# Summing one batch's fp32 log gates with fp32 matmuls, and reading the upper halves of the others as a strided view

## The chip, the cores and the metric

The kernel runs on one core of a Trainium2 chip. The metric is the device time of one execution in microseconds (us), lower is better. A time is a median over the executions named with it. "PE" is the TensorE matmul unit and "PEld" its weight loads, "DVE" is VectorE, "ACT" is ScalarE, "POOL" is GpSimd. A chunk is 128 time steps; a batch has 6 of them.

## The reference

Inputs are q, k, v and f_logit of shape 4 x 8 x 768 x 48 (batch, heads, time, head dimension), and four weight matrices. A gated linear attention is followed by an MLP mixer:

```python
f = 1.0 / (1.0 + np.exp(-f_logit))
state = np.zeros((B, H, D, D))
for t in range(S):
    state = f[:, :, t, :, None] * state + np.einsum('bhd,bhe->bhde', k[:, :, t], v[:, :, t])
    y[:, :, t] = np.einsum('bhd,bhde->bhe', q[:, :, t], state)
x = y.transpose(0, 2, 1, 3).reshape(4, 768, 384)

h = np.maximum(x.transpose(0, 2, 1) @ w_tok1, 0.0) @ w_tok2      # token mixing, 768 -> 256 -> 768
u = x + h.transpose(0, 2, 1)
h2 = np.maximum(u @ w_ch1, 0.0) @ w_ch2                          # channel mixing, 384 -> 1536 -> 384
return u + h2
```

## The kernel before

The attention is done in chunks. With L = -log f, each chunk needs the prefix sums of L over its 128 steps (one matmul with an upper triangular matrix of ones) and, for every head dimension, the total over the chunk (a matmul with a column of ones). Both are sums of fp32 numbers, and PE takes longer for them in fp32. So the kernel splits L into a bf16 high half and a bf16 rest and sums the two into the same fp32 PSUM tile.

The gates of one group of chunks: one Exp, one Ln rounded to bf16, the same Ln again in fp32, and a subtraction on POOL or DVE, whichever the planner finds free.

```python
def gates(b, c0, c1, key):
    ...                                          # cut: views fb (fp32), hi and lo (bf16)
    a = add({"ACT": cost}, lambda e: nc.scalar.activation(fb, fb, AF.Exp, bias=0.0, scale=-1.0), ...)
    h = add({"ACT": cost}, lambda e: nc.scalar.activation(hi, fb, AF.Ln, bias=1.0, scale=1.0), ...)
    g = add({"ACT": cost}, lambda e: nc.scalar.activation(fb, fb, AF.Ln, bias=1.0, scale=1.0), key, [h])
    o = add({"POOL": 0.85 * n, "DVE": 0.4 * n + 0.08},
            lambda e: on(e).tensor_tensor(lo, fb, hi, ALU.subtract), key, [g, h])
```

The sums of one chunk. In the totals, the tile of L is the *stationary* operand (`lhsT`), and is loaded as weights (L280 below: a load of 128 x 128 before each matmul), for one column of output:

```python
def cumsum(e):
    ...                                          # cut: a PSUM bank; Sv are its first 384 columns
    nc.tensor.matmul(Sv, lhsT=tri_bf, rhs=Lhi[i][:, c, :, 0:D], start=True, stop=False)
    nc.tensor.matmul(Sv, lhsT=tri_bf, rhs=Llo[i][:, c, :, 0:D], start=False, stop=True)
    if c < NCH - 1:
        bh, bl = blk(Lhi[i][:, c]), blk(Llo[i][:, c])
        for hp in range(HP):                     # 4 pairs of heads
            o = pS[:, DM + hp:DM + hp + 1]
            nc.tensor.matmul(o, lhsT=bh[:, hp, :], rhs=ones_bf, start=True, stop=False)
            nc.tensor.matmul(o, lhsT=bl[:, hp, :], rhs=ones_bf, start=False, stop=True)
```

From these sums come decays exp(-S) and exp(S) for q and k, then transposes of both on PE, scores, a mask, the state update, and the readout (`py`) of y. The mixer follows: token mixing (`x_bf`, `h1T`), the tiles of u, their transposes (`uT`), and the two long channel matmuls (`pm<-uT` and `pm<-w_ch,zT`).

Nothing is issued in the order of the program text. Each operation is added to a plan with a guessed cost per engine, and `Plan.order()` simulates the engines greedily and fixes every engine's order before the kernel runs. That an engine waits in its order can be seen at POOL, which stood idle for 8.10 us before one subtraction, with loads behind it (below).

## Time and profile before

| | before |
|---|---|
| time, median of 4 runs (beside the changed kernel) | 193.61 us (193.45 to 193.84) |
| span of the profiled run | 192.0 us |
| PE busy | 170.5 us, 89% |
| DVE busy, ACT busy | 129.5 and 129.4 us, 67% each |
| readout of batch 0 ends | 31.8 us |
| first matmul from `uT` (channel mixing of batch 0) | 42.6 us |

The page of the profiled run, cut to the lines used here. The first is each engine's busy time. The rows show the busy share in 40 slices of 4.8 us, in tenths, and PEclk the granted PE clock, in tenths of full speed.

```profile
span 192.0 us, 4351 instructions
...
PE 170.5 (89%) x1668; PEld 105.4 (55%) x1668; DVE 129.5 (67%) x286; ACT 129.4 (67%) x292; POOL 81.0 (42%) x92
...
PE   0787896679999999999999899999998999999992
...
PEclk9999999957999999999999999999999999999999
```

PE is nearly full after slice 8, so whatever delays its long matmuls shows in the end time, and PE has holes only before. The clock row reads half only in slice 8.

The chain of waits, cut to pieces (start, length, what):

```profile
14.08 0.55 DVE Llo_80 L261
...
15.88 0.46 PE py L371 x7
...
21.14 0.46 PE py L371 x7
...
31.23 0.35 PE py L371 x7
...
101.08 6.33 DMA kT_92<-kh_88
```

The clock records in the packed trace begin at 24.8 us, and the row prints time without a record as 9. Where a time is from "the clock records", these are meant.

Two lines of the timeline (start, length, engine, line, what; in brackets the wait before and what ended it), a copy on DVE during POOL's two subtractions:

```profile
38.00 1.74 DVE L190 CAST u_bf<-u_nat_109 128x384 bf16<-128x384 f32 x1
...
37.89 3.34 POOL L261 TENSOR_TENSOR Llo_81<-f_sb_77,Lhi_79 128x768 bf16<-128x768 f32 x2 [8.10 <-ACT f_sb_77 L259]
```

The same copy, undisturbed, takes 0.35 us at 36.22 us. POOL had waited 8.10 us for ACT's Ln, with loads queued behind it in its order.

The groups of the sums (line, engine, operation, operands, shapes, count, then busy us and mean ns of one):

```profile
L461 PE MATMUL pm<-uT,w_ch_68 128*128 128x384 bf16 x288 | 54.5, 330 | 1.1 <-ACT zT L194 0.8 <-DVE zT L196 0.2
...
L274 PE MATMUL pS<-Lhi_79,tri_bf 128*128 128x384 bf16 x12 | 4.3, 358 | 0.0
...
L280 PEld LDWEIGHTS <-Lhi_78 128*128 128x128 bf16 x40 | 3.2, 103 | 2.8 <-issue 2.4
```

A weight load of a bf16 tile takes about 0.10 us. In steady flow it hides behind the matmuls: the second channel matmuls (L480) have 288 loads of 98 ns, 27.3 us in all, and PE is idle for 0.0 us before them.

### The profile page before, as it was taken

The page shows a single profiled execution, that of the slowest core. Times are in us where ns is not written, and L with a number is a line of the kernel's source. Part 1 is how long each engine was busy: PE and PEld are TensorE (multiplying, and loading weights), DVE is VectorE, ACT ScalarE, POOL GpSimd, SP SyncE. Part 2 cuts the span into 40 slices and gives each one's busy share as a digit, 9 for nine tenths or more (in the row PEclk, how much of TensorE's full clock was granted, in tenths as well). Part 3 has the DMA queues.
Part 4 walks back from the last instruction along what each step waited for, and adds up shares of the span by engine and source line. Part 5 has one row for each costly group of instructions (what it writes and reads, how often), then busy time and mean ns, then how long its engine had stood idle before and what let it go on. Part 6 is the DMA issues. An engine that isn't in the chain of part 4 may idle for free.

```text
span 192.0 us, 4351 instructions
## 1 busy us (share of the span) xinstructions
PE 170.5 (89%) x1668; PEld 105.4 (55%) x1668; DVE 129.5 (67%) x286; ACT 129.4 (67%) x292; POOL 81.0 (42%) x92
## 2 busy tenths in 40 slices
PE   0787896679999999999999899999998999999992
PEld 0455553346666666656555566565665654656560
DVE  4578888988899757988998973898673637200222
ACT  4999793987989959774899953257996122598000
POOL 7999992199992449993990300000000000000000
PEclk9999999957999999999999999999999999999999
DMA  8999999999999999999999343344532124310222
GB/s 105 162 149 143 141 216 194 196 101 107 112 192 195 167 122 171 180 199 155 180 144 115 58 82 113 103 85 130 84 64 48 41 85 100 78 70 2 81 86 82
DMA packets 102213, 23.23 MB, mean 121 GB/s; under 512 B 95312, under 2 KB 100992, under 8 KB 102192
## 3 DMA queue, kind: packets, MB, share of 16 engines
q0 software_dynamic: 78800, 13.77, 99.6%
q1 hardware_dynamic: 23392, 9.18, 21.1%
q8 instruction: 13, 0.21, 0.5%
q14 instruction: 8, 0.07, 0.1%
HBM read 25.17 MB, written 4.72 MB: 156 GB/s over the span
## 4 chain that ended last, share of the span: by engine, by line
PE 53%; DVE 18%; ACT 15%; DMA 6%; issue 4%; POOL 2%; DVEq 0%; POOLq 0%; ACTq 0%
PE pm L480 24%; PE pm L461 14%; DMA kT_92<-kh_88 3%; PE pm L407 3%; DMA k_sb_72<-in_k_dram 3%; PE pm L426 2%; ACT zT L194 2%; DVE u_bf L190 2%; PE py L371 1%; ACT state_bd_103 L188 1%; DVE Am_96 L337 1%; DVE Am_95 L337 1%; DVE u_nat_109 L430 1%; ACT u_bf L188 1%; ACT state_bd_102 L188 1%
## 5 line engine op out<-in xcount | busy, mean ns | idle before, releaser
L461 PE MATMUL pm<-uT,w_ch_68 128*128 128x384 bf16 x288 | 54.5, 330 | 1.1 <-ACT zT L194 0.8
L480 PE MATMUL pm<-w_ch_69,zT 128*128 128x384 bf16 x288 | 50.5, 326 | 0.0
L194 ACT ACTIVATE zT<-pm 128x384 bf16<-128x384 f32 x73 | 34.7, 500 | 6.2 <-PE pm L461 5.8
L480 PEld LDWEIGHTS <-zT 128*128 128x128 bf16 x288 | 27.3, 98 | 17.7 <-issue 0.4
L461 PEld LDWEIGHTS <-w_ch_68 128*128 128x128 bf16 x288 | 26.3, 98 | 17.2 <-issue 2.6
L237 POOL DMA_DIRECT2D k_sb_72<-in_k_dram x12 | 11.0, 920 | 4.9 <-DMA f_sb_76<-in_f_logit_dram 4.9
L237 POOL DMA_DIRECT2D q_sb_70<-in_q_dram x12 | 11.2, 932 | 4.4 <-DMA w_ch_69<-in_moe_w_ch_dram 3.6
L196 DVE TENSOR_SCALAR zT<-pm 128x384 bf16<-128x384 f32 x23 | 12.2, 551 | 1.2 <-PE pm L461 1.2
L237 POOL DMA_DIRECT2D k_sb_73<-in_k_dram x12 | 11.2, 932 | 3.7 <-DVE zT L196 3.7
L426 PE MATMUL pm<-h1T,w_tok_67 128*128 128x384 bf16 x48 | 10.9, 332 | 0.8 <-ACT h1T L194 0.4
L237 POOL DMA_DIRECT2D v_sb_75<-in_v_dram x12 | 11.3, 941 | 0.0
L237 POOL DMA_DIRECT2D v_sb_74<-in_v_dram x12 | 11.1, 926 | 0.4 <-issue 0.4
L237 POOL DMA_DIRECT2D q_sb_71<-in_q_dram x12 | 11.2, 936 | 0.0
L261 POOL TENSOR_TENSOR Llo_81<-f_sb_77,Lhi_79 128x768 bf16<-128x768 f32 x3 | 5.0, 1669 | 14.7 <-ACT f_sb_77 L259 14.7
L489 DVE TENSOR_TENSOR out_sb_114<-u_nat_110,pm 128x384 f32<-128x384 f32 x2 | 1.1, 550 | 14.1 <-PE pm L480 14.1
L274 PE MATMUL pS<-Lhi_78,tri_bf 128*128 128x384 bf16 x12 | 4.9, 409 | 4.8 <-POOL ident masks.py:197 4.8
L188 ACT CAST x_bf_106<-py 128x384 bf16<-128x384 f32 x10 | 4.8, 482 | 6.4 <-PE py L376 6.4
L190 DVE COPY x_nat_105<-py 128x384 f32<-128x384 f32 x8 | 4.5, 558 | 6.5 <-ACT x_bf_107 L188 6.4
L188 ACT CAST x_bf_107<-py 128x384 bf16<-128x384 f32 x8 | 3.9, 488 | 7.3 <-PE py L376 7.2
L190 DVE COPY x_nat_104<-py 128x384 f32<-128x384 f32 x9 | 5.0, 558 | 5.4 <-ACT x_bf_106 L188 5.4
L287 ACT ACTIVATE G_82<-pS 128x384 bf16<-128x384 f32 x12 | 5.9, 488 | 4.2 <-PE pS L281 4.1
L430 DVE TENSOR_TENSOR u_nat_109<-x_nat_104,pm 128x384 f32<-128x384 f32 x12 | 6.2, 550 | 3.6 <-PE pm L426 3.5
(237 smaller groups left out, 394.8 us busy)
## 6 DMA issues: line engine op xcount, KB each, us to landing
f_sb_77<-in_f_logit_dram POOLq DMA_DIRECT2D x2, 1152.0 KB, 12.1
f_sb_76<-in_f_logit_dram SPq DMA_DIRECT2D x6, 192.0 KB, 4.5
q_sb_70<-in_q_dram POOLq DMA_DIRECT2D x12, 96.0 KB, 5.7
k_sb_72<-in_k_dram POOLq DMA_DIRECT2D x12, 96.0 KB, 5.2
v_sb_74<-in_v_dram POOLq DMA_DIRECT2D x12, 96.0 KB, 5.2
w_ch_68<-in_moe_w_ch_dram POOLq DMA_DIRECT2D x1, 1152.0 KB, 15.5
q_sb_71<-in_q_dram POOLq DMA_DIRECT2D x12, 96.0 KB, 7.9
k_sb_73<-in_k_dram POOLq DMA_DIRECT2D x12, 96.0 KB, 6.1
```

What stands on the lines that cost most here:

```text
L188: nc.scalar.copy(dst, src)
L190: on(e).tensor_copy(dst, src)
L194: nc.scalar.activation(dst, src, AF.Relu, bias=0.0, scale=1.0)
L196: nc.vector.tensor_scalar(dst, src, 0.0, None, ALU.max)
L237: lambda e, dst=dst, src=src: nc.gpsimd.dma_start(out=dst[i][:, c], in_=chunk_of(src, b, c)),
L261: lambda e: on(e).tensor_tensor(lo, fb, hi, ALU.subtract), key, [g, h])
L287: return lambda e: nc.scalar.activation(dst.rearrange("t h d -> t (h d)"), t["pS"][:, 0:DM], AF.Exp, bias=0.0, scale=scale)
L407: nc.tensor.matmul(t["p"][:, 0:DM], lhsT=w_tok1[:, kt, rt * 128:(rt + 1) * 128], rhs=x_bf[i][:, kt, :], start=(kt == 0), stop=(kt == NCH - 1))
L426: nc.tensor.matmul(t["p"][:, 0:DM], lhsT=w_tok2[:, kt, tt * 128:(tt + 1) * 128], rhs=h1T[:, kt, :], start=(kt == 0), stop=(kt == 1))
L430: u = made["u", b, tt] = add({"DVE": 0.47}, lambda e, tt=tt, t=t: nc.vector.tensor_tensor(u_nat[i][:, tt, :], x_nat[i][:, tt, :], t["p"][: ...
L461: nc.tensor.matmul(t["p"][:, 0:384], lhsT=w_ch1[:, kt, cc * 128:(cc + 1) * 128], rhs=uT[:, kt, th * 384:(th + 1) * 384], start=(kt == 0), ...
L480: nc.tensor.matmul(t["p"][:, 0:DM], lhsT=zT[:, kt, tt * 128:(tt + 1) * 128], rhs=w_ch2[:, kt, :], start=(kt == 0), stop=(kt == NCC - 1))
```

## The change

The intent: drop the second Ln and, in batch 0, the subtraction too.

- One Ln writes L in fp32. The bf16 high half is not computed but *read*: a bf16 view of the fp32 tile with stride 2 picks the upper 16 bits. In batches 1 to 3 the rest is still computed and summed.
- In batch 0, where PE has holes, L is summed in fp32, without a split.
- The planner's costs are retuned, so the order of everything changes. It also puts filler matmuls (`warm`, whose result nobody reads) into gaps that it foresees on PE before 46 us, meant to keep the clock up. Two more chunks have q and k transposed by PE rather than by DMA, and `x_bf` is copied from `x_nat` in SBUF.

```diff
+    L = two([128, NCH, H, 64], FP32, "L")
+    Lhi = [tl.bitcast(BF16).rearrange("t c h (d two) -> t c h d two", two=2)[:, :, :, :, 1] for tl in L]
...
-        h = add({"ACT": cost}, lambda e: nc.scalar.activation(hi, fb, AF.Ln, bias=1.0, scale=1.0), ...)
-        g = add({"ACT": cost}, lambda e: nc.scalar.activation(fb, fb, AF.Ln, bias=1.0, scale=1.0), key, [h])
-        o = add({"POOL": 0.85 * n, "DVE": 0.4 * n + 0.08},
-                lambda e: on(e).tensor_tensor(lo, fb, hi, ALU.subtract), key, [g, h])
+        g = add({"ACT": cost}, lambda e: nc.scalar.activation(full, fb, AF.Ln, bias=1.0, scale=1.0), ...)
+        o = g if b == 0 else add({"POOL": 0.85 * n} if b == 3 else {"DVE": 0.4 * n + 0.08},
+                lambda e: on(e).tensor_tensor(lo, full, hi, ALU.subtract), key, [g])
...
+            if b == 0:
+                nc.tensor.matmul(Sv, lhsT=tri_f, rhs=L[i][:, c, :, 0:D], start=True, stop=True)
+                if c < NCH - 1:
+                    bl = blk(L[i][:, c])
+                    for hp in range(HP):
+                        nc.tensor.matmul(pS[:, DM + hp:DM + hp + 1], lhsT=bl[:, hp, :], rhs=ones_f,
+                                         start=True, stop=True)
+                return
...
-        s = made["S", b, c] = add({"PE": 0.56}, cumsum, key - 0.02,
+        s = made["S", b, c] = add({"PE": 0.56 if b else 1.1}, cumsum, key - 0.02,
...
-        made["xb", b, c] = add(either, lambda e: copy(e, x_bf[i][:, c, :], t["py"][:, 0:DM]), ...)
+        made["xb", b, c] = add({"DVE": 0.28, "ACT": 0.38}, lambda e: copy(e, x_bf[i][:, c, :], x_nat[i][:, c, :]), ...)
...
-    XBAR_QK = 16
+    XBAR_QK = 18
...
+    def warm(reps):
+        def fn(e):
+            p = bank("mix", "warm")
+            for _ in range(reps):
+                nc.tensor.matmul(p[:, 0:DM], lhsT=idle[:, 0:128], rhs=idle, start=True, stop=True)
```

Cut: the planner's code that sizes the fillers, a separate planner queue for DMA transposes, the clearing of the new tiles, smaller cost constants, and batch 1's gates, which are computed one chunk at a time instead of two and planned a little later.

More of the change, by code (lines that the diff above doesn't have):

```diff
@@ L15 @@
 class Plan:
-    LATE = {"PE": 0.32, "ACT": 0.24, "DVE": 0.24, "POOL": 0.3, "SP": 0.1, "Q": 2.0}
+    LATE = {"PE": 0.32, "ACT": 0.24, "DVE": 0.24, "POOL": 0.3, "SP": 0.1, "Q": 2.0, "X": 1.3}
     BANKS = {"att": 5, "mix": 3}
     WINDOW = 150
+    WARM = None
+    WARM_UNTIL = 46.0
     def __init__(self):
@@ L36, in order @@
         queues = {e: sorted((o for o in self.ops if e in o["eng"]), key=lambda o: o["key"])
-                  for e in ("PE", "ACT", "DVE", "POOL", "SP", "Q")}
+                  for e in ("PE", "ACT", "DVE", "POOL", "SP", "Q", "X")}
         free = dict.fromkeys(queues, 0.0)
@@ L80, in order @@
             t, o, e = best
+            if e == "PE" and self.WARM and free["PE"] < self.WARM_UNTIL and t - free["PE"] > 0.45:
+                t_, last = max(free["PE"], 1.3), taken["mix"][-self.BANKS["mix"]:]
+                held = self.ops[last[0]]["readers"] if len(last) == self.BANKS["mix"] else []
+                if all(r in ends for r in held):
+                    t_ = max([t_] + [visible[r] for r in held])
+                    one = 0.165 if t_ > 4.0 else 0.34
+                    reps = int((t - t_ - 0.1) * 0.8 / one)
+                    if reps > 0:
+                        w = self.add({"PE": one * reps}, self.WARM(reps), 0.0, bank="mix")
+                        taken["mix"].append(w)
+                        ends[w] = free["PE"] = t_ + one * reps
+                        visible[w], on[w] = ends[w], "PE"
+                        out.append((t_, "PE", self.ops[w]))
             n = o["n"]
@@ L83, in order @@
             visible[n] = ends[n] + self.LATE[e]
+            if e == "X" and free["Q"] > t:
+                visible[n] += 3.5
             on[n] = e
@@ L132 @@
     ones_bf = st([128, 1], BF16, "ones_bf")
+    idle = st([128, DM], BF16, "idle")
+    nc.vector.memset(idle, 0.0)
     nc.vector.memset(ones_bf, 1.0)
+    tri_f = st([128, 128], FP32, "tri_f")
+    ones_f = st([128, 1], FP32, "ones_f")
+    nc.vector.memset(ones_f, 1.0)
     tri4 = tri_bf.unsqueeze(1).broadcast_to((128, 4, 128))
@@ L145 @@
     f_sb = two([128, H, NCH, D], FP32, "f_sb")
-    Lhi = two([128, NCH, H, 64], BF16, "Lhi")
+    L = two([128, NCH, H, 64], FP32, "L")
     Llo = two([128, NCH, H, 64], BF16, "Llo")
@@ L165 @@
     out_sb = [st([128, DM], FP32, f"out_sb{n}") for n in range(NCH)]
-    for tl in (*Lhi, *Llo):
+    Lhi = [tl.bitcast(BF16).rearrange("t c h (d two) -> t c h d two", two=2)[:, :, :, :, 1] for tl in L]
+    for tl in (*L, *Llo):
         nc.vector.memset(tl[:, :, :, D:64], 0.0)
@@ L227, in load_f @@
         else:
-            m = swdge(lambda e: nc.gpsimd.dma_start(out=f_sb[i], in_=src), key, 2.28, 5.9, 0.3,
-                      [made.get(("lo", b - 2, c)) for c in range(NCH)], at)
+            m = swdge(lambda e: nc.gpsimd.dma_start(out=f_sb[i], in_=src), key, 2.28, 6.3, 0.3,
+                      [made.get(("ln", b - 2, c)) for c in range(NCH)], at)
             for c in range(NCH):
@@ L237, in load_qkv @@
                 lambda e, dst=dst, src=src: nc.gpsimd.dma_start(out=dst[i][:, c], in_=chunk_of(src, b, c)),
-                key, 0.89, 0.71, 1.0, [made.get((u, b - 2, c)) for u in users], at)
+                key, 0.89, 0.78, 1.0, [made.get((u, b - 2, c)) for u in users], at)
     def load_w(name, dst, src, key, us, units):
@@ L246, in crossbar @@
         n = add({"SP": 1.2}, lambda e: nc.sync.dma_start_transpose(out=dst, in_=src), key, deps)
-        return add({"Q": 0.7}, None, key, [n])
+        return add({"X": 0.1}, None, key, [n])
     def gates(b, c0, c1, key):
@@ L252, in gates @@
         fb = f_sb[i].rearrange("t h c d -> t c h d")[:, c0:c1]
+        full = L[i][:, c0:c1, :, 0:D]
         hi, lo = Lhi[i][:, c0:c1, :, 0:D], Llo[i][:, c0:c1, :, 0:D]
@@ L256, in gates @@
                 key, [made["f", b, c] for c in cs])
-        h = add({"ACT": cost}, lambda e: nc.scalar.activation(hi, fb, AF.Ln, bias=1.0, scale=1.0),
+        g = add({"ACT": cost}, lambda e: nc.scalar.activation(full, fb, AF.Ln, bias=1.0, scale=1.0),
                 key, [a] + [made.get(("S", b - 2, c)) for c in cs])
-        g = add({"ACT": cost}, lambda e: nc.scalar.activation(fb, fb, AF.Ln, bias=1.0, scale=1.0), key, [h])
-        o = add({"POOL": 0.85 * n, "DVE": 0.4 * n + 0.08},
-                lambda e: on(e).tensor_tensor(lo, fb, hi, ALU.subtract), key, [g, h])
+        o = g if b == 0 else add({"POOL": 0.85 * n} if b == 3 else {"DVE": 0.4 * n + 0.08},
+                lambda e: on(e).tensor_tensor(lo, full, hi, ALU.subtract), key, [g])
         for c in cs:
+            made["ln", b, c] = g
             made["lo", b, c] = o
@@ L276, in cumsum @@
             if c < NCH - 1:
-                bh, bl = blk(Lhi[i][:, c]), blk(Llo[i][:, c])
+                bh = Lhi[i][:, c].rearrange("t (hp par) dd -> t hp (par dd)", par=2)
+                bl = blk(Llo[i][:, c])
                 for hp in range(HP):
@@ L381, in attention @@
         either = {"ACT": 0.38, "DVE": 0.47}
-        made["xb", b, c] = add(either, lambda e: copy(e, x_bf[i][:, c, :], t["py"][:, 0:DM]),
-                               key + 0.03, [made.get(("t1", b - 2))], frees=y)
-        made["xn", b, c] = add(either, lambda e: copy(e, x_nat[i][:, c, :], t["py"][:, 0:DM]),
-                               key + 0.03, [made.get(("u", b - 2, c))], frees=y)
+        xn = made["xn", b, c] = add(either, lambda e: copy(e, x_nat[i][:, c, :], t["py"][:, 0:DM]),
+                                    key + 0.03, [made.get(("u", b - 2, c))], frees=y)
+        made["xb", b, c] = add({"DVE": 0.28, "ACT": 0.38}, lambda e: copy(e, x_bf[i][:, c, :], x_nat[i][:, c, :]),
+                               key + 0.03, [xn, made.get(("t1", b - 2))])
     def mixing(b, key0, span):
@@ L491, in mixing @@
                 kk, [half, made.get(("out", tt))], frees=first)
-            s = add({"SP": 0.1}, lambda e, tt=tt, o=o: nc.sync.dma_start(out=out_b[tt], in_=o), kk, [n])
+            s = add({"SP": 0.45}, lambda e, tt=tt, o=o: nc.sync.dma_start(out=out_b[tt], in_=o), kk, [n])
             made["out", tt] = add({"Q": 0.7}, None, kk, [s])
@@ L506, in masks @@
         make_upper_triangular(nc, tri_bf, val=1.0, diag=True)
+        make_upper_triangular(nc, tri_f, val=1.0, diag=True)
         make_identity(nc, ident)
@@ L510 @@
         load_qkv(0, c, 0.1 * c)
-    load_w("w_tok1", w_tok1, moe_w_tok1, 0.60, 3.0, 0.75)
+    load_w("w_tok1", w_tok1, moe_w_tok1, 0.60, 3.3, 0.75)
     load_w("w_tok2", w_tok2, moe_w_tok2, 0.61, 2.2, 0.25)
@@ L528 @@
                     load_qkv(b + 1, c, b + 0.05 + 0.1 * c)
-            n = 2
+            n = 2 if b else 1
             for c in range(0, NCH, n):
-                gates(b + 1, c, c + n, b + 0.85 + LEAD[0] + LEAD[1] * c)
+                gates(b + 1, c, c + n, b + (0.85 if b else 0.95) + LEAD[0] + LEAD[1] * c)
                 for a in range(c, c + n):
@@ L534 @@
         mixing(b, b + 1.0, 1.0)
+    def warm(reps):
[3 more added lines that the diff above has]
+                nc.tensor.matmul(p[:, 0:DM], lhsT=idle[:, 0:128], rhs=idle, start=True, stop=True)
+        return fn
+    plan.WARM = warm
     order = plan.order()
```

## The prediction

> **What bounds it now.** Three stretches, read from engine activity by window and the timeline.
> (1) 0 to 31.5 us, batch 0's attention: ACT and DVE share the load, 75 to 97% and 81 to 85% busy from 10 to 30 us. POOL issues 18 q/k/v loads at 0.93 us each; DMA is full too.
> (2) 31.5 to 46 us: PE runs out of work (57% busy from 30 to 40 us), waiting on DVE for tiles of u and on DMA: batch 1's f_logit lands at 34.0 us, w_ch1 at 39.3 us. One u_bf copy takes 1.74 us on DVE under two POOL subtractions (3.34 us in sum; alone it takes 0.35). The granted clock is 0.50 from 38.3 to 45.6 us. [...]
> (3) From 46 us PE is 97% busy, but not all is work: the 288 matmuls from uT occupy 189 ns each, against 162 where nothing holds them (72 in 11.70 us, chain of waits at 165 us). PSUM evictions by the crowded ACT and DVE hold them.
>
> **What changes.**
> - One Ln per gate group goes: 6 of 0.52 us in batch 0, 0.83 us per two chunks after. ACT loses about 11 us, 3.1 of it in stretch 1.
> - Batch 0 loses its subtractions (4 DVE of 0.56, 2 POOL of 0.98 us). Batch 1's move to DVE (6 of 0.56), so no POOL work blocks the loads from 37.9 to 41.2 us or slows the copies.
> - Batch 0's sums become fp32: estimate 0.6 to 1.0 us per chunk against 0.55, on an idle PE.
> - x_bf is copied from SBUF (about 0.35 against 0.48 to 0.56 us), after x_nat.
> - The diff also carries filler matmuls in PE gaps foreseen before 46 us, and two more chunks transposed by PE instead of DMA: about +1 us of PE, but the 6.3 us DMA piece of the chain ending at 107 us goes.
> - Strided high halves: I expect no cost in matmul or weight load.
>
> **On the path.** Stretch 1: 6.4 us less on two engines, so it should end near 29 us. This doesn't pass through whole, because w_ch1 still lands at 38.5 to 39.3 us. But the two late tok2 pairs and first sums (1.8 us at full clock) get done before, and the long matmuls start 3 us sooner. A warm clock saves 2.7 us more (5.4 us at half rate); the order shows only one filler between u and the batch-1 sums, so I count half. Sum about 4.5 us. Later: ACT relief returns perhaps 1.5 us of the held matmuls (7.7 us held in all), less 1 us for transposes.
>
> Predicted 188.3 us, 80% range 184.5 to 191.5. Faster by over 2%: 0.74; within 2%: 0.23; slower: 0.03.
>
> **What would show it.** Readout of batch 0 ending near 29 us; first matmul from uT near 39 us (now 42.6); a clock of 1.00, or a dip under 4 us, between 36 and 46 us; POOL issuing loads from 34 us without a hole; ACT busy near 118 us (129.4), DVE level; matmuls from uT below 189 ns; strided sums at 160 to 165 ns.
>
> **What would make it wrong.** Fillers or fp32 sums delaying PE's real work in stretch 1; ACT, in order, blocked on batch 1's f_logit ahead of u copies; the clock falling anyway; strided reads slowing 18 sums by 160 ns each (+3 us); a new order leaving PE holes after 46 us.

The sum: about 4.5 us (3 us, and half of 2.7 us for the clock), then 1.5 us more and 1 us less, 5 us in all. The 2.7 us are worked out from the trace (5.4 us of PE work at a granted clock of 0.50); that fillers keep the clock up was assumed. The 0.6 to 1.0 us for fp32 sums is an estimate of mine that names no trace; the trace after has 1.5 to 3.14 us per chunk.

## The result, and the profile after

| | before | after |
|---|---|---|
| time, median of 4 runs | 193.61 us | 199.55 us (199.18 to 202.96; the last slow) |
| span of the profiled run | 192.0 us | 197.4 us |
| PE busy, PE idle | 170.5, 21.5 us | 181.5, 15.9 us |
| readout of batch 0 ends | 31.8 us | 37.4 us (predicted 29) |
| first matmul from `uT` | 42.6 us | 46.8 us (predicted 39) |

The change makes the kernel slower: 1.030 times the time before, 95% interval 1.028 to 1.032. A ratio here and below is the mean time of one kernel's fast runs over the mean of the fast runs of the kernel before in the same rounds, so it is not quite the ratio of the medians. The kernel before is run again in every batch of experiments, and its median there was between 193.7 and 194.2 us.

The page after:

```profile
span 197.4 us, 4449 instructions
...
PE 181.5 (92%) x1732; PEld 114.2 (58%) x1732; DVE 127.2 (64%) x287; ACT 124.9 (63%) x287; POOL 79.2 (40%) x92
...
PE   4999999678999999989998599999779999999992
...
PEclk9999999999999999999999999999999999999999
```

DVE and ACT got their relief, and PE has 5.6 us less idle time (21.5 - 15.9). But it has 11.0 us more busy time, so the span grew by 5.4 (the fillers are 12.1 us of the busy time, so this sum alone does not name a cause). The clock row shows no dip any more, and the clock records have full rate from 17.3 us on. PE has holes near 35 to 49 us (slices 7 to 9), near 110 us (slice 22) and from 138 to 148 us (slices 28 and 29); before, slices 9 and 28 and 29 were full.

The chain of waits after, cut:

```profile
5.21 1.65 PE pS L301 x2
6.86 1.50 PE pS L305 x8
8.35 0.98 PE warm L576 x3
...
18.38 0.84 PE pS L301 x2
19.22 0.79 PE pS L305 x8
...
27.06 1.73 PE warm L576 x10
...
33.02 0.35 PE py L406 x7
...
105.58 1.34 DVE state_105 L393
...
107.31 1.46 DVE state_bd_107 L215
...
142.85 3.95 DMA qT_96<-qh_92
```

The sums of batch 0 are now *in* the chain. L301 is the fp32 prefix sum, which the trace shows as two instructions. L305 is the totals: four matmuls, eight instructions, 1.50 us for four numbers per partition. One chunk's sums take 3.14 us (5.21 to 8.35), later 1.63 (0.84 + 0.79). The fillers are in the chain as well.

The groups of the sums after:

```profile
L496 PE MATMUL pm<-uT,w_ch_73 128*128 128x384 bf16 x288 | 53.1, 326 | 2.5 <-DVE zT L221 2.5
...
L576 PE MATMUL warm<-idle 128*128 128x384 bf16 x48 | 12.1, 389 | 1.5 <-DVE idle L152 1.1 <-ACT uT L213 0.3
...
L305 PEld LDWEIGHTS pS<-ones_f,L_83 128*128 128x128 f32 x40 | 7.1, 248 | 2.0 <-issue 1.2
L301 PE MATMUL pS<-L_83,tri_f 128*128 128x384 f32 x12 | 6.8, 653 | 2.0 <-POOL tri_f masks.py:66 2.0
L305 PE MATMUL pS<-ones_f,L_83 128*128 128x1 f32 x40 | 6.3, 278 | 0.0
...
L213 ACT CAST x_bf_111<-x_nat_109 128x384 bf16<-128x384 f32 x8 | 4.1, 510 | 0.2
...
L308 PE MATMUL pS<-L_84,tri_bf 128*128 128x384 bf16 x12 | 4.0, 337 | 0.0
```

The last line is a strided high half as the streamed operand: 337 ns, against 358 ns for the dense one before (L274), some of which fell into the clock's dip. The strided read is at least no slower. The fp32 weight load has a mean of 248 ns. Asked for by its source line, the trace gives minimum, median and maximum, here after and before:

```profile
L305 PEld LDWEIGHTS pS<-ones_f,L_83 x40: 190/192/337, 6.0 to 25.7; 128*128 128x128 f32 x40
```

```profile
L280 PEld LDWEIGHTS <-Lhi_78 x40: 95/100/151, 6.0 to 95.1; 128*128 128x128 bf16 x40
```

So an fp32 load takes 190 ns, or up to 337 ns early in the run, where a bf16 load takes 95, or 151. Each fp32 total has two of them (40 loads for 20 totals). These times overlap, so the pace is better read from the starts of the loads in the packed trace: within a chunk's totals, the next fp32 load starts after 112 ns at full rate and 213 ns before 17 us, the next bf16 load after 25 to 28 ns (h2 below, and before). Seven such steps make 0.78 and 1.49 us, nearly the whole time of the eight.

Three windows in which PE is short of work after (window, its length, then busy us and instructions of PE, PEld, DVE, ACT and POOL, then granted clock, DMA share (packet times added up, so it can pass 1) and GB/s):

```profile
35.00:40.00 5.00, 3.47 (x34) 1.92 (x34) 1.85 (x3) 2.17 (x6) 2.28 (x3) 1.00 2.33 151
...
105.00:110.00 5.00, 3.50 (x33) 1.98 (x32) 4.88 (x6) 4.24 (x11) 5.00 (x6) 1.00 2.13 111
...
140.00:145.00 5.00, 4.10 (x54) 2.54 (x51) 3.40 (x9) 4.00 (x10) 0.00 (x0) 1.00 0.55 110
```

PE is busy for 3.47, 3.50 and 4.10 of 5 us. In the first none of the other engines is even half busy: PE waits for batch 0's chain, which ends late; in the second DVE and POOL are full.

POOL's remaining subtractions, of batch 3, in the timeline:

```profile
99.33 1.47 POOL L286 TENSOR_TENSOR Llo_86<-L_84 128x768 bf16<-128x768 f32 x1 [12.56 <-ACT L_84 L283]
...
108.65 2.98 POOL L286 TENSOR_TENSOR Llo_86<-L_84 128x768 bf16<-128x768 f32 x2
```

The hole that the change removes from POOL at 38 us reappears at 99 us and longer (12.56 us of waiting, where it was 8.10). Two slow DVE operations are in the chain of waits at 105 to 109 us: 1.34 us for a step of the state and 1.46 us for a copy of it, where the same lines take 0.36 and 0.26 us elsewhere in this trace (0.52 for a pair of copies). The first of them (105.58 to 106.92 us) lies beside POOL issuing loads, the second beside the start of POOL's subtraction only (108.65); the next copy of the state, 108.78 to 110.31 us, takes 1.53 us and lies wholly beside it. So these lines alone don't show the subtraction to be the cause. An experiment below does more.

### The profile page after: what moved, and what is told of

It reads as the page before. It is cut to its first block, busy times and chain, and to the rows that moved or that the text cites. A ratio compares the mean times of both kernels' runs of the same rounds, so it can differ in the third digit from the quotient of the medians.

```text
span 197.4 us, 4449 instructions
## 1 busy us (share of the span) xinstructions
PE 181.5 (92%) x1732; PEld 114.2 (58%) x1732; DVE 127.2 (64%) x287; ACT 124.9 (63%) x287; POOL 79.2 (40%) x92
## 4 chain that ended last, share of the span: by engine, by line
PE 68%; DVE 11%; ACT 10%; DMA 5%; issue 3%; POOL 2%; POOLq 0%; DVEq 0%
PE pm L515 21%; PE pm L496 17%; PE warm L576 4%; PE pS L301 3%; PE pm L442 3%; PE pS L305 3%; PE py L406 2%; PE pq L342 2%; DVE u_nat_115 L465 2%; DMA qT_96<-qh_92 2%; PE pd L382 2%; PE pk L342 2%; PE pm L461 2%; ACT L_84 L283 2%; PE py L411 1%
## 5 line engine op out<-in xcount | busy, mean ns | idle before, releaser
L496 PE MATMUL pm<-uT,w_ch_73 128*128 128x384 bf16 x288 | 53.1, 326 | 2.5 <-DVE zT L221 2.5
L219 ACT ACTIVATE zT<-pm 128x384 bf16<-128x384 f32 x76 | 36.5, 493 | 12.1 <-PE pm L496 12.0
L576 PE MATMUL warm<-idle 128*128 128x384 bf16 x48 | 12.1, 389 | 1.5 <-DVE idle L152 1.1
L221 DVE TENSOR_SCALAR zT<-pm 128x384 bf16<-128x384 f32 x20 | 10.9, 551 | 1.6 <-PE pm L496 1.5
L322 ACT ACTIVATE G_87<-pS 128x384 bf16<-128x384 f32 x12 | 5.9, 489 | 7.5 <-PE pS L316 3.8
L286 POOL TENSOR_TENSOR Llo_86<-L_84 128x768 bf16<-128x768 f32 x3 | 4.4, 1517 | 12.6 <-ACT L_84 L283 12.6
L301 PE MATMUL pS<-L_83,tri_f 128*128 128x384 f32 x12 | 6.8, 653 | 2.0 <-POOL tri_f masks.py:66 2.0
L322 ACT ACTIVATE G_88<-pS 128x384 bf16<-128x384 f32 x12 | 5.9, 491 | 3.9 <-PE pS L305 3.4
L305 PEld LDWEIGHTS pS<-ones_f,L_83 128*128 128x128 f32 x40 | 7.1, 248 | 2.0 <-issue 1.2
L213 ACT COPY x_nat_110<-py 128x384 f32<-128x384 f32 x7 | 3.4, 488 | 6.8 <-PE py L411 6.8
## 6 DMA issues: line engine op xcount, KB each, us to landing
f_sb_81<-in_f_logit_dram SPq DMA_DIRECT2D x6, 192.0 KB, 4.8
```

Source lines behind the costliest of these rows:

```text
L219: nc.scalar.activation(dst, src, AF.Relu, bias=0.0, scale=1.0)
L221: nc.vector.tensor_scalar(dst, src, 0.0, None, ALU.max)
L301: nc.tensor.matmul(Sv, lhsT=tri_f, rhs=L[i][:, c, :, 0:D], start=True, stop=True)
L305: nc.tensor.matmul(pS[:, DM + hp:DM + hp + 1], lhsT=bl[:, hp, :], rhs=ones_f, start=True, stop=True)
L322: return lambda e: nc.scalar.activation(dst.rearrange("t h d -> t (h d)"), t["pS"][:, 0:DM], AF.Exp, bias=0.0, scale=scale)
L496: nc.tensor.matmul(t["p"][:, 0:384], lhsT=w_ch1[:, kt, cc * 128:(cc + 1) * 128], rhs=uT[:, kt, th * 384:(th + 1) * 384], start=(kt == 0), ...
```

## The experiments

The question is where the expected gain of 5 us and a loss of 6 us came from. Theory A: the fp32 sums are on batch 0's chain and cost several us. Rival B: the fillers stand ahead of real work. Rival C: the new order as such, above all batch 3's subtractions on POOL, makes holes later. Rival D: the strided view or the single Ln. All experiments give results within the reference's tolerance. Runs of one group ran on the same chip with the same runs of the kernel before. A trace is of one execution, and the clock differs between executions.

### One change alone, in the order of the kernel before

**f1_strided.** One Ln, in fp32, and the strided high half in all batches; the split stays everywhere. The plan is not touched: the operation removed is replaced by nothing, so each engine keeps its order.

```diff
-    h: nc.scalar.activation(hi, fb, AF.Ln, ...)
+    h: None
-    g: nc.scalar.activation(fb, fb, AF.Ln, ...)
+    g: nc.scalar.activation(full, fb, AF.Ln, ...)      # hi is the strided view of full
```

> The kernel before, with its order of instructions kept: one Ln into an fp32 tile in place of two, the high half read as a strided view, the bf16 split kept in all batches, batch 0 too; no fillers, no fp32 sums, no other part of the change. If the loss comes from fp32 sums, fillers or the new order (my theory), this is 0.5 to 2.5 us faster than before, about 192: the ACT load falls, the order does not. If strided reads or the lost Ln cost something, it is slower than 193.6.

Measured: 194.47 us (193.91 to 195.18), ratio 1.002 (0.996 to 1.008). One Ln per group less on ACT gains nothing, and strided reads cost nothing, to within the interval. This refutes rival D as a cause of 3%, and it speaks against my prediction's view of the first stretch: with less work on ACT, batch 0's readout ended at 35.3 us, not earlier than the 31.8 before. One caution: by the clock records PE reached full rate at 33.1 us in this execution, and at 24.8 in that of the kernel before, so the later readout may be the clock's.

**f2_fp32.** f1 and, in batch 0, fp32 sums and no subtraction. This is the change that was named, alone.

```diff
+    if b == 0: matmul(Sv, lhsT=tri_f, rhs=L);  4 x matmul(pS[:, DM+hp], lhsT=blk(L), rhs=ones_f);  return
-    o: lo = full - hi
+    o: None if b == 0
```

> The same, with batch 0 summed in fp32 without subtraction: the named change alone, in the order of before. Theory fp32 (on a half-rate PE the fp32 sums take 3 us a chunk and sit on the chain): 2 to 5 us slower than the strided version, the readout of batch 0 ends after 33 us (31.7 before). Rival (fillers alone delay batch 0): within 1 us of the strided version.

Measured: 201.84 us (201.27 to 202.79), ratio 1.040 (1.034 to 1.047). It costs 7.4 us against f1 (201.84 - 194.47), with no filler and no new order. Its chain of waits, cut, and below it f1's for the sums of two chunks and a readout:

```profile
5.21 1.65 PE pS L280 x2
6.85 1.50 PE pS L284 x8
8.35 1.49 PE pS L280 x2
...
31.28 1.50 PE pS L284 x8
...
41.01 0.35 PE py L385 x7
```

```profile
15.14 0.43 PE pS L276
15.58 0.32 PE pS L277
...
16.09 0.34 PE pS L276
...
27.58 0.46 PE py L374 x7
```

In f1 a chunk's sums take 0.95 us of the chain (15.14 to 16.09); in f2 3.14 us (5.21 to 8.35). Theory A is confirmed for the named change. The fp32 weight loads of f2 never reach the fast value:

```profile
L284 PEld LDWEIGHTS pS<-ones_f,L x40: 333/333/338, 6.0 to 32.4; 128*128 128x128 f32 x40
```

**i1_hitotals.** f2, but the totals alone are taken from the bf16 high half. This is a cruder sum on purpose (no rest is added), only to separate the totals from the prefix sums, which stay fp32.

```diff
-    bl = blk(L[i][:, c]);                              matmul(..., lhsT=bl[:, hp, :], rhs=ones_f)
+    bl = Lhi[i][:, c].rearrange("t (hp par) dd -> ...");  matmul(..., lhsT=bl[:, hp, :], rhs=ones_bf)
```

> The version with fp32 sums in the order of before (201.8), with batch 0's column totals taken from the bf16 high half alone, so 4 bf16 matmuls a chunk in place of 8 fp32 passes over fp32 weights; the prefix sums stay fp32. The totals are cruder on purpose. If the totals' weight loads (about 1.5 us a chunk at half rate) are half of the fp32 cost: 3 to 4 us faster, 197.5 to 199. If the cost is the prefix sums (or latency elsewhere): within 1.5 us of 201.8.

Measured: 194.30 us (194.06 to 195.16), ratio 1.004 (1.000 to 1.007). The whole cost of f2 is gone, more than the 3 to 4 us that I expected. Its chain of waits at one chunk:

```profile
24.06 1.58 PE pS L280 x2
25.64 0.09 PE pS L284 x4
```

The totals take 0.09 us instead of 1.50 (four bf16 loads instead of eight fp32 ones; f1's eight bf16 totals take 0.19, 15.90 to 16.09 us). Five chunks times 1.41 us is 7.05 us, and all five stand in f2's chain; f2 minus i1 is 7.5 us (201.84 - 194.30, two groups of runs). So the cost of the named change is the totals: fp32 tiles loaded as weights for one column of output each. What pays for the fp32 prefix sums in i1 is not shown: four of 1.49 to 1.59 us stand in its chain, 6.2 us, where f1's has three of 0.66 to 0.75, and no subtraction stands in f1's chain before 46 us. The clock records differ too (i1 is at full rate from 8.7 to 12.1, from 18.9 to 22.4 and from 29.2 us).

### The fillers

**g2_fill.** The kernel before with fillers only: 11 at the start, 3 after each transpose of u in batch 0.

```diff
+    fill(bank("mix", "warm"), 11)
 ...
+                if b == 0:
+                    fill(bank("att", "warm"), 3)
```

> The kernel before, same order and same operations, with filler matmuls added alone: 11 before the first sum (PE waits there for its masks) and 3 after each transpose of a tile of u in batch 0. Theory clock (PE runs at half rate through most of batch 0 and again from 38 to 46 us, and batch 0's chain passes through PE): both halves shorten, readout of batch 0 ends by 31 us, no dip at 38 to 46 us, time 189 to 192. Rival (batch 0 bound by ACT and DVE work, dip unimportant because DMA holds the start of the long matmuls): 193 to 194.

Measured: 192.95 us (192.57 to 193.85), ratio 0.994 (0.988 to 1.001). It removes the dip of the clock near 40 us and gains about 1 us; the interval holds 0 and 2.3 us. I had counted half of 2.7 us for this. It is not a clean test of the dip: by the clock records PE is at full rate from 5.1 to 8.5 us and then at half rate until 29.0, which is 4 us later than before.

**g3_stridedfill.** f1 with the fillers of g2.

```diff
+    fillers of g2_fill on f1_strided
```

> The kernel before, same order, with both the single Ln and strided view and the fillers of the run with fillers alone (which gave 0.994 of before). If the Ln taken away pays once PE runs at full rate: 1 to 3 us faster than fillers alone, 190 to 192. If ACT's Ln was never on the chain of batch 0: within 0.8 us of it, about 193.

Measured: 193.74 us (193.40 to 194.34), ratio 1.000 (0.997 to 1.004). Strided view, one Ln and fillers together bring nothing in the order before.

**e1_nofill.** The changed kernel in exactly its order, with fillers not issued.

```diff
     def fn(e):
-        p = bank("mix", "warm")
-        for _ in range(reps):
-            nc.tensor.matmul(p[:, 0:DM], lhsT=idle[:, 0:128], rhs=idle, start=True, stop=True)
+        return
```

> The changed kernel, same order, filler matmuls not issued. Theory fp32: gains at most 2 us (197.5 to 199.5), batch 0 readout still ends after 35 us, and the clock may fall to half again. Rival, fillers: gains 4 us or more (195.5 or less), readout before 34 us. If both matter: between.

Measured: 203.64 us (202.74 to 205.72), ratio 1.051 (1.042 to 1.059). The fillers *help* the changed kernel, by 2%, although they are in its chain; neither of my two expectations had that. Rival B falls as the cause of the loss. Why they help can be read from how long PE stays slow: by the durations of equal matmuls and by the clock records alike, to about 17 us with fillers and to about 37 us without, and fp32 totals take 1.50 us in the slow state and 0.79 in the fast one.

**e2_split0.** The changed kernel in its order, fillers kept, batch 0 summed with the bf16 split again (subtraction on DVE just after the Ln).

```diff
+    if b == 0: nc.vector.tensor_tensor(lo, full, hi, ALU.subtract)      # with the Ln
-    if b == 0: fp32 sums
+    if False:  fp32 sums
```

> The changed kernel, same order, fillers kept, batch 0 summed with the bf16 split as other batches (subtraction on DVE). Theory fp32: readout of batch 0 ends 3 to 5 us sooner (33 us) and the time falls by 2 to 4 us (195.5 to 197.5). Rival, fillers: at most 1 us. A second rival, that the order after 50 us (batch 3 subtractions on POOL, PE holes at 105 to 115 and 135 to 150 us) makes the loss: batch 0 ends sooner but the time falls by less than 1 us.

Measured: 199.16 us (197.09 to 199.72), ratio 1.023 (1.014 to 1.032). Less than 1% came back, far from what f2 against f1 says. Part of this may be the clock: three of the four runs have a mean clock of 0.972 to 0.974 and take 198.93 us or more, the fourth, at 0.999, takes 197.09; in the profiled run the rate is half again from 22.6 to 26.0, from 43.1 to 46.5 and from 111.4 to 114.8 us.

**e3_both.** e1 and e2 together: no fillers, split in batch 0.

```diff
+    the edits of e1_nofill and of e2_split0
```

> The changed kernel, same order, no fillers and batch 0 with the bf16 split. Theory clock and fp32: without fillers PE stays at half rate to 30 us or later; the split takes away 11 us of PE work at that rate, so it is faster than the version with fp32 sums and no fillers (203.6) by 3 us or more, about 199 to 201, and slower than the split version with fillers (199.2) by 0 to 2. If the split is worth under 1 us here too, as it was with fillers, fp32 sums are not the cause in this order.

Measured: 196.77 us (195.15 to 198.58, the last slow), ratio 1.011 (1.002 to 1.019). Without fillers, fp32 sums cost 4.0% in this order too (1.051 against 1.011). With them, the same step is worth 0.7% (1.030 against 1.023): fillers take back part of the fp32 cost, and themselves cost 1.2% where there is no fp32 sum to speed up (1.023 against 1.011). (These ratios are of different groups of runs, each to the kernel before on its own chip run, the intervals of 1.030 and 1.023, and of 1.023 and 1.011, overlap, and e2's clock may be in both differences.) By these values the two effects are not additive.

### The order and batch 3's subtractions

**e4_sub3dve.** The changed kernel in its order, with batch 3's three subtractions on DVE instead of POOL.

```diff
-    lambda e: on(e).tensor_tensor(lo, full, hi, ALU.subtract)
+    lambda e: nc.vector.tensor_tensor(lo, full, hi, ALU.subtract)
```

> The changed kernel with one thing altered, in the same order: batch 3's three subtractions are done by DVE instead of POOL. Theory late order (POOL waits 12.6 us for ACT with the loads of batch 3 behind it, and its subtraction slows DVE copies to 1.3 and 1.5 us at 106 to 110 us): 2 to 4 us faster than the changed kernel (195.5 to 197.5), and the PE hole at 105 to 115 us goes. Rival (startup alone made the loss): within 1 us of 199.5.

Measured: 198.15 us (197.37 to 198.47), ratio 1.020 (1.013 to 1.026). They cost 1.0% of the 3.0, less than the 2 to 4 us that I expected: rival C is a part of the loss. The two slow DVE operations are gone: no state operation on DVE takes over 0.95 us for a pair. They are there again in e3_both, which keeps the subtractions on POOL (1.34 us, and 3.00 for a pair of copies).

**h1_replan.** The changed kernel with the split in batch 0 and the plan made for it (cost 0.56 for the sums).

```diff
-    o = g if b == 0 else add({"POOL": 0.85 * n} if b == 3 else {"DVE": 0.4 * n + 0.08}, ...)
+    o = add({"POOL": 0.85 * n} if b == 3 else {"DVE": 0.4 * n + 0.08}, ...)
-    "PE": 0.56 if b else 1.1
+    "PE": 0.56
```

> The changed kernel with batch 0 split in bf16 and its order planned anew with that cost (0.56 us of PE, subtraction on DVE); all other parts of the change stay. If fp32 sums, and the order planned around a too small cost for them, made the loss, this is at or below before: 189 to 194. If the rest of the change (POOL subtractions in batch 3, transposes, fillers) makes it, it stays at 196 to 199.

Measured: 194.79 us (193.19 to 196.76, the last slow), ratio 1.000 (0.991 to 1.009). Batch 0 is now early (readout ended at 30.5 us, first matmul from `uT` at 40.4), but the gain is lost later: batch 2's token mixing starts 5.7 us earlier than before, batch 3's 0.5 us later.

**h2_replan_d3.** h1 with batch 3's subtractions planned on DVE.

```diff
-    {"POOL": 0.85 * n} if b == 3 else {"DVE": 0.4 * n + 0.08}
+    {"DVE": 0.4 * n + 0.08}
```

> The replanned split version (1.000 of before), with batch 3's subtractions planned on DVE. Theory late order: the hole at 105 to 115 us and the slow DVE copies under POOL go, 1 to 3 us faster: 191 to 193. Rival: DVE gets 3 us more work in batch 3's attention and loses what POOL gave: 194 to 196.

Measured: 189.35 us (188.68 to 192.21, the last slow), ratio 0.975 (0.971 to 0.980). The rest of the change, without fp32 sums and without subtractions on POOL, beats both kernels. Its page:

```profile
span 187.5 us, 4462 instructions
...
PE 172.4 (92%) x1737; PEld 106.3 (57%) x1737; DVE 126.3 (67%) x287; ACT 126.7 (68%) x296; POOL 75.1 (40%) x89
```

PE is busy 172.4 us, 9.1 less than in the changed kernel (181.5).

**j4_again.** h2 once more, in more rounds.

```diff
     (no edit against h2_replan_d3)
```

> The replanned split version with DVE subtractions once more, on this chip, with more rounds: 0.970 to 0.982 of before if the first result holds.

Measured: 190.21 us (189.07 to 191.70, 6 runs), ratio 0.983 (0.978 to 0.988). It is faster than before in both groups, by 1.7 to 2.5%; the runs fall near 189.2 and near 191.5, and I don't know why.

**h3_u3.** h2 with batch 2's u also transposed by PE instead of DMA.

```diff
-    XBAR_U = 2
+    XBAR_U = 3
```

> As the replanned split version with batch 3's subtractions on DVE, and batch 2's u transposed by PE instead of DMA, so that the DMA transposes of batch 3's q and k do not stand behind six transposes of u (8 us on the queue). If PE's holes at 135 to 150 us (2.2 us in the changed kernel) come from that queue: 1 to 2 us faster than its sibling. If PE's 1 us more of transposes and the evictions eat it: same or slower.

Measured: 191.83 us (190.62 to 193.45), ratio 0.991 (0.984 to 0.998). Slower than h2 in the same group (0.975), so my hope for the DMA queue fails. By how much it is worse is unsure: the slowest run, which is the profiled one, ran at a clock of 0.95 from 9.9 us on; the other three have a mean of 191.4 us. That PE loses more by the transposes than DMA frees is not shown.

**j3_nofill.** h2, same order, fillers not issued.

```diff
+    the edit of e1_nofill on h2_replan_d3
```

> The replanned split version with DVE subtractions (189.4 us, 0.975 of before), same order, fillers not issued. Theory clock (fillers bring PE to full rate at 5 us and keep it there to 50 us): 2 to 6 us slower, 191 to 195, with half rate to 20 us or later. If the order alone made the gain: within 1 us of it.

Measured: 190.97 us (190.83 to 191.63), ratio 0.987 (0.983 to 0.991), beside 0.983 for h2 in the same group. The intervals overlap: with bf16 sums, fillers matter little, although PE stays slow to about 29 us without them and, in the two traces with them (h2 and j4), only to 4.2 and 8.9 us.

### The totals in the order of the changed kernel

**j1_after_hitot.** The changed kernel, its own order and fillers, with totals from the high half as in i1.

```diff
+    the edit of i1_hitotals on the changed kernel
```

> The changed kernel in its own order, with batch 0's column totals from the bf16 high half alone (cruder on purpose); fp32 prefix sums, fillers, order, POOL subtractions kept. In the order of before this took away the whole fp32 cost. Theory totals: 3 to 6 us faster than the changed kernel (199.5), at 193.5 to 196.5; what is left over before is the late order (about 2 us of POOL subtraction in batch 3). Rival (in this order fillers, planned for another clock, hold batch 0 as much): 197 or more.

Measured: 196.76 us (194.38 to 198.82, the last slow), ratio 1.009 (1.002 to 1.015). The median lies between my two expectations; the mean of the three fast runs, 195.96, is within the first. The totals account for 2.1% of the 3.0 (1.030 against 1.009, from different groups).

**k1_tot_sub3.** j1 and e4 together: fast totals, batch 3's subtractions on DVE, the order and the fillers as in the changed kernel.

```diff
+    the edits of i1_hitotals and of e4_sub3dve on the changed kernel
```

> The changed kernel in its own order with two things altered: batch 0's column totals from the bf16 high half, and batch 3's subtractions on DVE. Alone they gave 1.009 and 1.020 of before against 1.030. If the two make up the whole loss and add: 0.995 to 1.003 of before, 193 to 194.5. If something else in the order is left: 1.005 or more.

Measured: 192.92 us (192.28 to 194.38), ratio 0.995 (0.989 to 1.001). The two parts together close the loss: the changed kernel's own order is no slower than before once the slow totals and POOL's subtractions are out of it. The two hide one another a little: the totals are worth 2.5% with the subtractions on DVE (1.020 against 0.995), and the subtractions 1.4% with fast totals (1.009 against 0.995), where alone it was 2.1 and 1.0%.

**k2_tot_sub3_nofill.** k1 without fillers.

```diff
+    the edit of e1_nofill on k1_tot_sub3
```

> The same without fillers. With the slow totals fillers gained 2%, with the split they cost 1.3%, in the replanned order they gained 0.4%. If fillers only pay where PE's own work is long at half rate: 0 to 1.3% faster than with them (0.985 to 1.000). If they pay whenever the clock is low: 0.5 to 2% slower.

Measured: 192.30 us (190.66 to 196.13), two of the four runs slow; the two fast ones (190.66 and 191.05) give 0.983 (0.979 to 0.987). On two fast runs this is thin (the third, 193.54, counts as slow by little, 1.5% above the fastest), but it has the sign of e2 against e3: in this order, fillers cost about 1.2% when there is nothing slow for them to speed up.

**j2_fp32_d3.** fp32 prefix sums with fast totals, planned anew (cost 0.85), batch 3's subtractions on DVE: a test of whether the idea pays with the totals mended.

```diff
+    the edit of i1_hitotals;  {"DVE": 0.4 * n + 0.08} for b >= 1;  "PE": 0.56 if b else 0.85
```

> As the version above, with the order planned anew (0.85 us of PE for a chunk of batch 0) and batch 3's subtractions on DVE. If fp32 prefix sums without subtraction are worth having once the totals are cheap: 0.5 to 2 us faster than the replanned split version with DVE subtractions (189.4), 187.5 to 189. If not: 189 to 192.

Measured: 191.37 us (190.90 to 191.70), ratio 0.988 (0.984 to 0.992). In the same group h2 again had 0.983. Even with mended, too crude totals, fp32 prefix sums are not better than the split.

## Why the prediction was wrong

I predicted 188.3 us and gave slower by over 2% a chance of 0.03. It was 199.55 us.

**The step that failed: "Batch 0's sums become fp32: estimate 0.6 to 1.0 us per chunk against 0.55, on an idle PE."** Measured: 3.14 and 2.78 us for the first two chunks, 1.5 to 1.7 after about 17 us, and not on an idle PE but in the chain of waits: from 10 to 20 and from 20 to 30 us PE was busy for 7.75 and 8.79 of 10 us even before the change, and for 10.00 and 9.92 after it. Three things were missed in this one term.

1. *The weight load.* I had counted columns that stream past. But in the totals the fp32 tile is the weight, and one column streams. Each of the 4 totals becomes two instructions with a load each: eight fp32 loads, one every 112 ns, or every 213 ns in the slow state, where bf16 loads follow each other after 25 to 28 ns. A load takes 192 ns in fp32 (after, median) and 100 ns in bf16 (before, median); why it takes longer, no run separates. Experiment i1 shows that it is the totals and not the prefix sums: with bf16 totals the 7.4 us are gone. That their loads set the pace is read from the trace.
2. *Two instructions for each fp32 matmul.* The trace shows two of them; the prefix sum takes 0.75 to 0.91 us in the fast state and 1.28 to 1.65 in the slow one. With both bf16 halves it takes 0.44 us in h2's fast state (0.28 + 0.16) and 0.75 us in f1's slow state (0.43 + 0.32). This doubling is real, and yet i1 comes out even with f1; why, no run shows.
3. *The slow state.* I looked for it at the dip at 38 us and not at the start, because the clock row read 9 there. The trace speaks against the row: equal readouts take 0.46 us at 15.88 and 21.14 us and 0.35 us at 31.23 us in the kernel before, whose first clock record is the switch to full rate at 24.8 us. In f2 the records begin at 35.8 us. There the clock row (below) reads 9 in slices 0 to 9 (up to 50 us), while the same eight instructions take 1.50 us at 6.85 and at 31.28 us, and 0.79 us in the fast state after the change. In i1 the records do give half rate, from 22.4 to 29.2 us, and a prefix sum takes 1.58 us in it, at 24.06 us; before f2's first record it takes 1.49 to 1.65 us. What brings the slow state on and what ends it is not shown. In the kernel before, PE was busy for 3.09 us of the 5 us before the dip (33.45 to 38.45) and for all of the 5 us before full rate came back (40.28 to 45.28); but in f2 PE reads 80% busy or more from 5 to 25 us (row below), and the slow state lasts to 35.8 us.

```profile
PE   0989969974999999999999999999998999999992
...
PEclk9999999999799999999999999999999999999999
```

**The second wrong step: "6.4 us less on two engines, so it should end near 29 us."** I read shares of 75 to 97% on ACT and 81 to 85% on DVE as a throughput bound. (My own items make 5.3 us on the two engines, 3.1 + 4 x 0.56, not 6.4.) It is a latency chain, in turn through DVE, PE, ACT and DMA. The Exp and Ln operations are not in it: of the gates, only one subtraction of 0.55 us at 14.08 is. f1 agrees: an Ln less per group changed nothing (1.002), and with fillers it gained nothing either (g3, 1.000, against 0.994 for the fillers alone in g2).

**A third part: the new order moves POOL's hole and does not remove it.** I had looked only at batch 1's subtractions. Batch 3's are fixed to POOL by the change, with batch 3's loads queued behind them. e4 prices them at 1.0%, k1 against j1 at 1.4%. That POOL's subtractions also slow DVE, the traces show in part: before, a copy took 1.74 us inside POOL's subtractions and 0.35 us outside; after, operations of 1.34 to 1.53 us on the state between 100 and 115 us appear only in kernels that keep the subtractions on POOL, though the first of them does not overlap a subtraction in the trace. A copy of 1.32 us at 49.8 us in j3, which has no subtraction on POOL, shows that these are not the only cause of slow DVE operations. How much of the 1.0% is this and how much the 12.56 us for which POOL held the loads back, no run separates.

How the pieces come together is best seen in the milestones of the profiled runs, in us. "uT" is the first matmul from `uT` in batch 0, "tok" the start of token mixing, "end" the last channel matmul; in brackets the difference to before.

| | uT, batch 0 | tok, batch 2 | tok, batch 3 | end |
|---|---|---|---|---|
| before | 42.6 | 117.3 | 153.0 | 188.3 |
| f1, one Ln, strided | 45.7 (+3.1) | 118.6 (+1.3) | 154.4 (+1.4) | 189.7 (+1.4) |
| f2, with fp32 sums | 52.0 (+9.4) | 124.7 (+7.4) | 160.5 (+7.5) | 195.7 (+7.4) |
| i1, bf16 totals | 44.7 (+2.1) | 117.8 (+0.5) | 153.6 (+0.6) | 188.8 (+0.5) |
| after | 46.8 (+4.2) | 119.2 (+1.9) | 159.6 (+6.6) | 193.9 (+5.6) |
| e4, after with batch 3 on DVE | 47.1 (+4.5) | 117.8 (+0.5) | 158.3 (+5.3) | 192.6 (+4.3) |
| j1, after with bf16 totals | 41.8 (-0.8) | 116.3 (-1.0) | 157.6 (+4.6) | 191.9 (+3.6) |
| k1, j1 with batch 3 on DVE | 41.4 (-1.2) | 112.5 (-4.8) | 153.3 (+0.3) | 187.6 (-0.7) |
| h2, split and replanned | 40.1 (-2.5) | 109.3 (-8.0) | 149.8 (-3.2) | 184.0 (-4.3) |

In the order of before, a delay of batch 0 is carried to the end nearly whole: f2's +6.3 us at uT against f1 is +6.0 at the end. In the changed order this depends on what comes later: of the 5.0 us that j1 wins at uT against the changed kernel only 2.0 reach the end while POOL keeps batch 3's subtractions, but with them on DVE k1's 5.7 us against e4 arrive as 5.0.

The changed kernel loses at two places, in batch 0 (the totals; j1 wins back 5.0 us there) and before batch 2's and batch 3's token mixing (POOL; k1 wins back another 3.8 and 4.3 us). There is a gain in what is left of the change: h2, planned anew without these two costs, runs at 189.35 and 190.21 us. That this is near the 188.3 predicted is luck. h2 keeps a subtraction in batch 0, so it is not the kernel that I reasoned about, and the part that I counted on most, relief of ACT, gave nothing alone (f1, g3). Which of the new order, the two more chunks transposed by PE, the `x_bf` copies and the fillers makes h2's gain, no run separates; j3 says that most of it is not the fillers.

**What held.** Strided reads cost nothing that shows, for streaming (337 ns against 358) and as weights (a load takes 96 to 97 ns after, L315, against 100 to 103 before, L280; f1: 1.002). The clock row has no dip near 40 us. POOL's hole at 38 us is gone, though from 34 to 37.6 us POOL still waits, now for the transfer of `w_ch1` (4.38 us in all). The matmuls from `uT` occupy less than 189 ns each (53.1 us over 288 is 184).

**What else missed.** ACT is busy 124.9 us, not 118: `x_bf` copies on ACT take 510 ns from SBUF, where I had estimated 0.35 us, which holds on DVE alone, and there in one of two groups (0.36 and 0.46). The fillers of g2, which take the dip away, gained about 1 us, near the half of 2.7 that I had counted, but the dip is not alone in that difference. `w_ch1` landed at 37.3 us and was not what the long matmuls waited for: batch 0 itself came later.

**What stays open.**
- The fillers do three different things in three comparisons: +2.0% of gain with slow totals (e1 against after), about even in h2's order, and a cost of about 1.2% in the changed kernel's order without slow totals. That they bring the fast state forward (17.3 us against 36.9 in e1), and that fp32 totals gain most from that, fits; that they delay work behind them in order is argued, not shown.
- h2 is 8.0 us early at batch 2's token mixing and only 3.2 us at batch 3's. Something limits batch 3's attention. DMA transposes of up to 3.95 us are in the chain there after, and in h2 PE waits 0.68 and 1.63 us for `kT` from DMA at 129.0 and 134.3 us, but no run separates them.
- f1's uT comes 3.1 us later than before with no later loss of that size. Its late switch to full rate (33.1 us against 24.8) may be the cause; with one trace of each kernel this is not shown.
- When PE reaches full rate differs from trace to trace (35.8 us in f2, 8.7 at first in i1, 10.5 in k1). How much of the cost of the totals is their own length, and how much a later full rate, no run separates.

## What to carry to other kernels

Before you trade a bf16 split for fp32, ask for every matmul which operand is the weight: here an fp32 tile as the stationary operand for one column of output took two loads of 190 to 338 ns, and a chunk's totals eight loads and 1.50 us in the slow state (0.79 in the fast one), where the split's eight bf16 totals took 0.19. Low use of an engine is not slack if its work is a link of a latency chain: look for the engine's own pieces in the chain of waits, and compare equal instructions at different times, because a clock row may not show that the early ones run slow (here it printed time before the first record as full). When a change re-plans everything, run its parts in the old order first: the named part cost 7 us there, and the gain was in the rest.
